# Score units against the last chunk at 448 columns, with the doubled half block squared again by VectorE

## The chip, the cores and the metric

The kernel runs on one core of one Trainium2 chip. The metric is device time in microseconds (us). The kernel before takes 1192.46 us (median of three runs, 1191.73 to 1192.65).

Engines are named as the profile names them: PE is TensorE, DVE is VectorE, ACT is ScalarE, POOL is GpSimd, SP is SyncE (here a DMA queue). PEld is PE's loading of weights, which overlaps its matmuls.

## The reference

```python
# u, v: (8, 3008, 256); z: (8, 3008, 64); w_in: (256, 2048); w_out: (2048, 256)
scores = matmul(z, z.transpose(0, 2, 1)) / S        # S = 3008
attn   = maximum(scores, 0.0) ** 2
x      = (u * matmul(attn, v)).reshape(B * S, D)
h      = x @ w_in
out    = (h / (1 + exp(-1.702 * h))) @ w_out
```

The scores are symmetric, since both factors are z. The kernel uses this: it computes many blocks once, and transposes them ("turns" them) by DMA for use on the other side of the diagonal.

## The kernel before

The 3008 tokens of a batch are cut into six chunks of 512; the last has 448 tokens, and its last block of 128 rows holds the 64 remaining tokens twice. A score unit is two key blocks (2 x 128) against the queries of one chunk. PE computes it in two row tiles of 64 rows that run side by side, ACT applies Relu, and DVE squares. In the code below, `CB` = 4 blocks make a chunk, `NCH` = 6 chunks and `NU` = 12 pairs of key blocks make a batch; `i` is a chunk of queries, `jp` a pair of key blocks. `...` marks lines left out.

```python
LAST = S - (NCH - 1) * CH      # 448
LFULL = LAST - SREM            # 384

def turned(b, i):              # units of chunk i against the last chunk's queries
    return i < NCH - 1 and (b > 0 or i > 3)

def scores(b, group):
    ...
        turn = turned(b, i) and jp >= NU - 2
        kp, qi = (2 * i + jp - (NU - 2), NCH - 1) if turn else (jp, i)
        m = CB // 2 if folded(b, i) and jp == 2 * i + 1 else CB
        for r in range(2):
            h = slice(r * DQK, (r + 1) * DQK)
            pe.matmul(sc[:, r, :m * P], zt[h, 2 * kp + r, :],
                      zt[h, (qi + 1) * CB - m:(qi + 1) * CB, :], start=True, stop=True)

def square(b, i, jp, sc):
    ...
    act.activation(rl, sc, AF.Relu, scale=csc)
    ...
    dve.tensor_tensor(a, rl, rl, ALU.mult)
    if jp // 2 > i and (turned(b, i) or jp < NU - 2):
        if b and i == 0 and LATE:
            late.append(((jp + 2) % NU, lambda: turn_unit(b, i, jp, a)))
        else:
            turn_unit(b, i, jp, a)         # sp.dma_start_transpose into a "tt" tile
```

Of the kernel before, what the change touches and what calls it, by code (L numbers as in the profile page):

```python
# [11 lines left out]
P = 128  # L12
# [3 lines left out]
def kernel(  # L16
# [13 lines left out]
    AF = mybir.ActivationFunctionType  # L30
    ALU = mybir.AluOpType
# [8 lines left out]
    CH = 512  # L40
    NCH = (S + CH - 1) // CH
    CB = CH // P
    NU = NJ // 2
# [6 lines left out]
    LAST = S - (NCH - 1) * CH  # L50
    LFULL = LAST - SREM

    csc = 16.0
    FSC = csc * csc * float(S) * float(S)

    dve, act, pe, sp, pool = nc.vector, nc.scalar, nc.tensor, nc.sync, nc.gpsimd
# [126 lines left out]
    def width(i):  # L183
        return CH if i < NCH - 1 else LAST
# [28 lines left out]
    def folded(b, i):  # L213

        return i < NCH - 1 and b > 0

    def turned(b, i):

        return i < NCH - 1 and (b > 0 or i > 3)

    def scores(b, group):
        scs = []
        zt = ZT[b]
        for i, jp in group:
            sc = ps2.tile([P, 2, CH], F32, name="sc", tag="ps2")
            turn = turned(b, i) and jp >= NU - 2
            kp, qi = (2 * i + jp - (NU - 2), NCH - 1) if turn else (jp, i)
            m = CB // 2 if folded(b, i) and jp == 2 * i + 1 else CB
            for r in range(2):
                h = slice(r * DQK, (r + 1) * DQK)  # L230
                pe.matmul(  # L231
                    sc[:, r, :m * P], zt[h, 2 * kp + r, :], zt[h, (qi + 1) * CB - m:(qi + 1) * CB, :],
                    start=True, stop=True,
                )
            scs.append(sc)
        return [lambda u_=u_, sc=sc: square(b, *u_, sc) for u_, sc in zip(group, scs)]

    def square(b, i, jp, sc):
        rl = pw.tile([P, 2, CH], F16, name="rl", tag="rl", bufs=3)
        if folded(b, i) and jp == 2 * i + 1:  # L240
            rh = rl[:, :, :CH // 2]
            act.activation(rh, sc[:, :, :CH // 2], AF.Relu, scale=csc)
            dve.tensor_tensor(unit[b, i, jp][:, 1], rh, rh, ALU.mult)
            return
        act.activation(rl, sc, AF.Relu, scale=csc)  # L245
        if folded(b, i) and jp == 2 * i:
            a = pa.tile([P, CB, 2, P], F16, name="a", tag="a", bufs=26)
            unit[b, i, jp] = a
            r4 = rl.rearrange("p r (q c) -> p r q c", q=CB)
            dve.tensor_tensor(a.rearrange("p q r c -> p r q c"), r4, r4, ALU.mult)  # L250
            unit[b, i, jp + 1] = pa.tile([P, 2, 2, CH // 2], F16, name="ad", tag="a", bufs=26)
            sp.dma_start_transpose(
                unit[b, i, jp + 1][:, 0].rearrange("p g (r c) -> p (g r) c", c=P),
                a[:, CB // 2:].rearrange("p q r c -> p (q r c)"),
            )
            return
        a = pa.tile([P, 2, CH], F16, name="a", tag="a", bufs=26)
        unit[b, i, jp] = a
        dve.tensor_tensor(a, rl, rl, ALU.mult)  # L259
        if jp // 2 > i and (turned(b, i) or jp < NU - 2):  # L260
            if b and i == 0 and LATE:
                late.append(((jp + 2) % NU, lambda: turn_unit(b, i, jp, a)))
            else:
                turn_unit(b, i, jp, a)

    def turn_unit(b, i, jp, a):
        cj = jp // 2
        if (b, i, cj) not in TT:
            TT[b, i, cj] = pa.tile([P, CB, CB, P], F16, name="tt", tag="tt", bufs=14)
        k0 = 2 * (jp % 2)  # L270
        sp.dma_start_transpose(
            TT[b, i, cj][:, k0:k0 + 2].rearrange("p r g c -> p (r g) c"),
            a.rearrange("p r c -> p (r c)"),
        )
# [309 lines left out]
    def take(b, n):  # L584
        for post_ in scores(b, [queue.pop(0) for _ in range(n)]):
            post_()
# [17 lines left out]
    for copies in [first_zt(g) for g in range(2)]:  # L604
        copies()
    posts = scores(0, [queue.pop(0) for _ in range(2)])
    turns = []
    for g in (2, 3):
# [8 lines left out]
    for b in range(B):  # L617
# [3 lines left out]
        turn, load = (TURN, LOAD) if b else (TURN0, LOAD0)  # L621
# [92 lines left out]
```

## Time and profile before

| | value | where it is read |
|---|---|---|
| time, span | 1192.46 us, 1190.8 us | times, page |
| PE busy | 1183.7 us, 99% | busy table |
| DVE busy, ACT busy | 820.6 us, 830.5 us | busy table |
| score matmuls in the chain that ended last | 6% | chain of waits |
| PE waiting for other engines | 3.3 us, all in the start | list of waits |

The page's busy table gives each engine's busy time, its share of the span and its instructions:

```profile
PE 1183.7 (99%) x11427; PEld 722.6 (61%) x11427; DVE 820.6 (69%) x1315; ACT 830.5 (70%) x987; POOL 231.9 (19%) x325
```

The page's chain that ended last, by engine and by line (L331 output matmuls, L372 and L473 the feed-forward part, L231 scores):

```profile
PE 98%; ACT 0%; DMA 0%; DVE 0%; issue 0%; SPq 0%; ACTq 0%
PE o L331 40%; PE hg L372 27%; PE st L473 23%; PE sc L231 6%; PE yp L529 2%; DMA zf<-in_z_dram 0%; ACT rl L245 0%; DVE zst L126 0%; DVE a L259 0%; ACT ZT L141 0%; ACT zst L124 0%; DVE y L489 0%; SPq L109 0%; PE zp L133 0%; ACTq L245 0%
```

The list of waits of PE (who waited for whom, us in total, times, longest):

```profile
PE w L97 <- DVE nil L75: 1.2, 1, 1.2
PE zp L133 <- DVE zst L126: 1.2, 2, 0.8
PE sc L231 <- ACT ZT L141: 0.9, 3, 0.4
```

PE is busy nearly throughout, waits only at the very start, and is itself nearly the whole chain. So PE's own columns set the time.

The timeline of PE at 238 us (start, us, engine, line, output and inputs, shapes, count) shows what a pair costs. The 18 output matmuls of 64x448 start at 238.19 and the next scores at 239.90, which is 1.71 us for nine pairs, 190 ns a pair. The score pair of 64x512 starts at 237.98 and what follows it at 238.19.

```profile
237.98 0.38 PE L231 MATMUL sc<-ZT 64*128 64x512 f16 x2
238.19 1.86 PE L331 MATMUL o<-a,V 64*128 64x448 f16 x18
239.90 0.59 PE L231 MATMUL sc<-ZT 64*128 64x512 f16 x4
```

The groups of instructions, shapes kept apart (count, busy us, mean ns of one, idle time before them), for Relu (L245, L242) and squares (L259, L243):

```profile
L245 ACT ACTIVATE rl<-sc 128x1024 f16<-128x1024 f32 x309 | 303.5, 1027 | 150.3 <-PE sc L231 147.5 <-DVE a L259 0.8
L259 DVE TENSOR_TENSOR a<-rl 128x1024 f16<-128x1024 f16 x274 | 188.7, 693 | 158.5 <-ACT rl L245 158.1 <-DMA tt<-a 0.4
L242 ACT ACTIVATE rl<-sc 128x512 f16<-128x512 f32 x35 | 21.5, 614 | 7.3 <-PE sc L231 7.3
L243 DVE TENSOR_TENSOR ad<-rl 128x512 f16<-128x512 f16 x35 | 14.7, 420 | 5.9 <-ACT rl L242 5.4
```

### The profile page before, as it was taken

The numbers are of one execution on the slowest core, as the hardware profiler recorded it, in microseconds if no ns is written. First come the engines' busy times: TensorE is split into PE (matmuls) and PEld (weight loads), VectorE is DVE, ScalarE is ACT, GpSimd is POOL, SyncE is SP. The second block draws the span as 40 slices with busy tenths as digits, with TensorE's granted clock in tenths as the row PEclk, the third lists the DMA queues.
The fourth block names the chain that finished last, engine by engine and source line by source line (L and its number), as shares of the span: only waits on it lengthen the run. The fifth ranks groups of instructions, "written<-read, shape, count | busy, mean of one in ns | idle before, by whom it ended". The sixth has DMA issues, their size and how long they took to land.

```text
span 1190.8 us, 27541 instructions
## 1 busy us (share of the span) xinstructions
PE 1183.7 (99%) x11427; PEld 722.6 (61%) x11427; DVE 820.6 (69%) x1315; ACT 830.5 (70%) x987; POOL 231.9 (19%) x325
## 2 busy tenths in 40 slices
PE   8999999999999999999999999999999999999998
PEld 3446765467754676546765478554775547855577
DVE  6788755777757775587765877558776487664776
ACT  7887865688656886478864787657876578672785
POOL 5243100331012320133101331014200142001000
PEclk9999999999999999999999999999999999999999
DMA  9996567666787667856778558886579855695012
GB/s 230 175 137 110 127 138 130 86 112 134 143 132 79 107 141 151 130 68 102 158 140 131 72 95 159 157 112 89 104 128 164 115 88 109 138 165 96 1 37 72
DMA packets 373021, 141.80 MB, mean 119 GB/s; under 512 B 315424, under 2 KB 366368, under 8 KB 372896
## 3 DMA queue, kind: packets, MB, share of 16 engines
q1 hardware_dynamic: 314256, 96.77, 45.1%
q0 software_dynamic: 57280, 42.03, 23.0%
q8 instruction: 89, 1.46, 0.5%
q10 hardware_dynamic: 1360, 1.25, 0.3%
q14 instruction: 36, 0.29, 0.1%
HBM read 60.29 MB, written 24.64 MB: 71 GB/s over the span
## 4 chain that ended last, share of the span: by engine, by line
PE 98%; ACT 0%; DMA 0%; DVE 0%; issue 0%; SPq 0%; ACTq 0%
PE o L331 40%; PE hg L372 27%; PE st L473 23%; PE sc L231 6%; PE yp L529 2%; DMA zf<-in_z_dram 0%; ACT rl L245 0%; DVE zst L126 0%; DVE a L259 0%; ACT ZT L141 0%; ACT zst L124 0%; DVE y L489 0%; SPq L109 0%; PE zp L133 0%; ACTq L245 0%
## 5 line engine op out<-in xcount | busy, mean ns | idle before, releaser
L380 ACT ACTIVATE gf<-hg 128x1024 f32<-128x1024 f32 (+1 forms) x384 | 385.8, 1005 | 138.0 <-PE hg L372 114.7
L245 ACT ACTIVATE rl<-sc 128x1024 f16<-128x1024 f32 x309 | 303.5, 1027 | 150.3 <-PE sc L231 147.5
L331 PEld LDWEIGHTS <-V 64*128 64x128 f16 (+1 forms) x4052 | 239.6, 94 | 235.4 <-issue 13.0
L372 PE MATMUL hg<-xt,W 128*128 128x512 f16 (+1 forms) x1408 | 354.6, 374 | 0.0
L384 DVE TENSOR_SCALAR gt<-gf 128x1024 f16<-128x1024 f32 (+1 forms) x320 | 223.2, 698 | 136.8 <-ACT gf L380 134.1
L331 PE MATMUL o<-a,V 64*128 64x512 f16 (+3 forms) x2286 | 303.8, 369 | 0.0
L259 DVE TENSOR_TENSOR a<-rl 128x1024 f16<-128x1024 f16 x274 | 188.7, 693 | 158.5 <-ACT rl L245 158.1
L193 POOL DMA_DIRECT2D uq<-in_u_dram x188 | 128.5, 691 | 612.2 <-PE sc L231 329.1
L331 PE MATMUL o<-tt,V 64*128 64x512 f16 (+1 forms) x1510 | 234.4, 377 | 0.0
L372 PEld LDWEIGHTS <-W 128*128 128x128 f16 x1536 | 139.3, 98 | 119.3 <-issue 2.6
L473 PEld LDWEIGHTS <-gt 128*128 128x128 f16 x2816 | 169.5, 98 | 31.8
L473 PEld LDWEIGHTS <-s 128*128 128x128 f16 x2112 | 127.8, 98 | 25.3 <-issue 0.3
L231 PE MATMUL sc<-ZT 64*128 64x512 f16 (+1 forms) x688 | 121.6, 367 | 1.2 <-ACT ZT L141 0.9
L473 PE MATMUL st<-WT,gt 128*128 128x128 f16 x1408 | 93.0, 219 | 0.0
L473 PE MATMUL st<-WT,s 128*128 128x128 f16 x1408 | 92.3, 219 | 0.0
L473 PE MATMUL st<-W,gt 128*128 128x128 f16 x1408 | 92.3, 219 | 0.0
L489 DVE SCALAR_TENSOR_TENSOR y<-st,uP 128x256 f32<-128x256 f32 x132 | 55.0, 419 | 21.6 <-PE st L473 10.9
L382 ACT ACTIVATE gt<-gf 128x1024 f16<-128x1024 f32 (+1 forms) x64 | 66.0, 1031 | 2.1
L348 DVE TENSOR_TENSOR xt<-o,ut 128x512 f16<-128x512 f32 x80 | 51.4, 683 | 22.7 <-PE o L331 22.7
L231 PEld LDWEIGHTS <-ZT 64*128 64x128 f16 x688 | 39.0, 94 | 45.0 <-issue 9.1
L483 ACT ACTIVATE uP<-st 128x256 f32<-128x256 f32 x132 | 49.7, 377 | 23.2 <-PE st L473 11.2
L446 DVE TENSOR_TENSOR s<-s,gt 128x1024 f16<-128x1024 f16 x88 | 60.3, 685 | 1.0
(51 smaller groups left out, 618.2 us busy)
## 6 DMA issues: line engine op xcount, KB each, us to landing
out_dram<-y SPq DMA_DIRECT2D x40, 512.0 KB, 3.3
uq<-in_u_dram POOLq DMA_DIRECT2D x156, 128.0 KB, 3.6
V<-in_v_dram POOLq DMA_DIRECT2D x35, 256.0 KB, 6.7
tt<-a SPq DMA_TRANSPOSE x232, 3.8
uq<-in_u_dram POOLq DMA_DIRECT2D x32, 112.0 KB, 5.2
vst<-in_v_dram SPq DMA_DIRECT2D x3, 512.0 KB, 5.8
out_dram<-y POOLq DMA_DIRECT2D x4, 384.0 KB, 3.2
zst<-in_z_dram POOLq DMA_DIRECT2D x7, 192.0 KB, 8.2
```

The source lines that it names most:

```text
L193: eng.dma_start(uq[k * QW:(k + 1) * QW, :n // QW].rearrange("t q c k -> t q (c k)"), src[:, :, cs])
L231: pe.matmul(sc[:, r, :m * P], zt[h, 2 * kp + r, :], zt[h, (qi + 1) * CB - m:(qi + 1) * CB, :], start=True, stop=True,)
L245: act.activation(rl, sc, AF.Relu, scale=csc)
L259: dve.tensor_tensor(a, rl, rl, ALU.mult)
L331: ins = pe.matmul(acc[c][:, :n], V16[b][h, j].rearrange("p (c k) -> p k c", k=NCC)[:, c], weights(b, i, j)[h], start=(k, m) == first[c], s ...
L372: pe.matmul(hg[:, e, :n], W1[:, c, ff * P:(ff + 1) * P], XT[b, i][:, c, :n], start=(c == 0), stop=(c == NCC - 1),)
L380: act.activation(gf[:, :, :n], hg[:, :, :n], AF.Gelu_apprx_sigmoid, scale=1.0 / FSC)
L382: act.activation(g, gf[:, :, :n], AF.Copy, scale=FSC)
L384: dve.tensor_scalar(g, gf[:, :, :n], FSC, None, ALU.mult)
L446: dve.tensor_tensor(s_, ST[b, k, "S1", h], a11, ALU.subtract)
L473: pe.matmul(bank[:, m, :], lhs()[:, f, m, :], right[:, ff, :], start=name in ("P1", "P2", "P5") and m == 0 and ff == 0, stop=ff == NFF // ...
L489: dve.scalar_tensor_tensor(y[:, :, o, c], ST[b, k, "bank" + x], 1.0 / FSC, ST[b, k, "after" + u_], ALU.mult, ALU.add,)
```

## The change

A unit against the last chunk's queries has only 448 different columns; the kernel before computes 512, the last 64 twice. The change computes 448. Where the unit is turned, the doubled half block is still needed by the transpose, and DVE squares it a second time out of the same Relu output.

```diff
-            m = CB // 2 if folded(b, i) and jp == 2 * i + 1 else CB
+            q0, q1 = qi * CH, qi * CH + width(qi)
+            if folded(b, i) and jp == 2 * i + 1:
+                q0 += CH // 2
             for r in range(2):
                 h = slice(r * DQK, (r + 1) * DQK)
                 pe.matmul(
-                    sc[:, r, :m * P], zt[h, 2 * kp + r, :], zt[h, (qi + 1) * CB - m:(qi + 1) * CB, :],
+                    sc[:, r, :q1 - q0], zt[h, 2 * kp + r, :], zt[h].rearrange("d n p -> d (n p)")[:, q0:q1],
                     start=True, stop=True,
                 )
@@
-        act.activation(rl, sc, AF.Relu, scale=csc)
+        turn = turned(b, i) and jp >= NU - 2
+        n = width(NCH - 1 if turn else i)
+        act.activation(rl[:, :, :n], sc[:, :, :n], AF.Relu, scale=csc)
@@
-        dve.tensor_tensor(a, rl, rl, ALU.mult)
+        dve.tensor_tensor(a[:, :, :n], rl[:, :, :n], rl[:, :, :n], ALU.mult)
+        if turn:
+            twice = rl[:, :, LFULL:LAST]
+            dve.tensor_tensor(a[:, :, LAST:], twice, twice, ALU.mult)
```

## The prediction

> **What bounds the kernel.** TensorE, almost everywhere. The page's busy table gives PE 1183.7 us of a span of 1190.8 (99%), DVE 820.6, ACT 830.5. The chain that ended last is 98% PE; score matmuls (line 231) are only 6.2%. In the list of waits PE waits for other engines for 3.3 us in all, every time in the start. The granted clock is 0.999. So PE is paced by its own columns: in the chain, 50 output matmuls of 64x512 (25 pairs; the two row tiles of a pair run side by side) take 5.40 us, 216 ns a pair. In the timeline at 238 us, 9 pairs of 64x448 take 1.71 us, 190 ns a pair. This agrees with the Trainium skill, "TensorE: Matmul & The Clock Gate", section "Wait — 56ns, not 53.3ns?": N / 2.4 GHz + about 2.5 ns between matmuls, here per pair.
>
> **What the change does.** The instruction order shows 96 score units (192 of 688 score matmuls) going from 512 to 448 columns: 72 turned units (10 in each of batches 1 to 7, 2 in batch 0) and 24 units of the last chunk as its own queries. The number of PE instructions does not change.
> - PE: 96 x (216 - 189.5) = 2.5 us less, all on the chain. All 96 stand among row-tiled output pairs, so no mode of the array changes.
> - ACT: Relu over 896 instead of 1024 elements. From 1027 ns for 1024 and 614 for 512 the slope is 0.807 ns: 0.10 us less each, about 10 us of busy time in all. Off the chain.
> - DVE: the square of 1024 takes 693 ns, of 512 takes 420: slope 0.53 ns, fixed part about 147 ns. The 896-wide square should take 625 ns, the added 128-wide one about 215. A turned unit then costs about 840 ns (+147), a last-chunk unit 625 (-68): 72 x 147 - 24 x 68 = +9 us, so DVE goes to about 830 us. Off the chain.
> - DMA transposes of turned units: same number and size, each starting some 0.05 us later. No wait of PE for a transpose is in the list of waits, so this should be hidden.
>
> **On the critical path.** Only the 2.5 us of PE columns (0.2%). The doubled squaring costs nothing unless DVE is late somewhere.
>
> **Predicted time: 1190.0 us**, 8 times in 10 within 1188.9 to 1191.5. Chances: faster by over 2% 0.005, within 2% 0.985, slower by over 2% 0.01. Faster by something: 0.9, since the three runs before spread by only 0.9 us.
>
> **What would show it.** Right: span and PE busy both lower by about 2.5 us; 192 score matmuls of 64x448, start to start 190 ns per pair; PE waits unchanged, none for DVE or a transpose; DVE busy about +9 us with 72 squares near 215 ns; ACT about -10 us. Wrong: PE busy down by 2.5 us but the span less, with PE waiting for DVE squares, transposed tiles or a score bank; or 64x448 score pairs still at 216 ns, because a weight load (94 ns each, two per pair) or the semaphore wait in front of a pair sets the pace.
>
> **What would make it wrong.** A place where the extra DVE instruction (about 0.15 us) holds the three-deep Relu buffer and so ACT, a score bank and PE: today ACT waits for a square only once, 0.8 us. Or the non-contiguous 2x448 operands costing DVE or ACT more than the slope says. Or the time outside the span (1192.46 against 1190.8) moving by as much as the gain.

## More of the kernel before

All transposes go through one queue, SP's, in the order in which `turn_unit` is called. And in chunk 2 of batch 0, PE reads the blocks of its own chunk first, then the turned ones of chunks 0 and 1, then the rest:

```python
def attend(b, i, both=False):
    ...
    if b == 0 and i == 2:
        js = js[own:own + CB] + js[:own] + js[own + CB:]
```

Last, a view that the prediction did not use. It is the view of the tile `tt`, the turned blocks, cut to its transposes (duration of an issue in ns, minimum, median, maximum) and to the time from issue to landing:

```profile
L271 SPq DMA_TRANSPOSE tt<-a x232: 1231/1288/5162, 10.3 to 1087.7; - x116
DMA to landing us min/median/max: 3.1/3.8/10.4
```

An issue usually holds the queue for 1.3 us and lands after 3.8 us, but some hold it for 5 us and land after 10. In the trace, the three slowest landings and the four longest issues are all of transposes issued in the first 56 us. PE did not wait for any of them in this one execution.

## The result, and the profile after

The changed kernel took 1192.36 us (median of six runs, 1189.90 to 1196.78), the kernel before 1192.51 (six runs, 1191.72 to 1192.87). The ratio is 1.0003, with a 95% interval of 0.998 to 1.0027. A ratio here is the mean time of one kernel's fast runs over that of the other's of the same rounds, so it is not quite the ratio of the medians. The median lies outside the predicted range of 1188.9 to 1191.5.

The six runs are not spread around 1192.4, though. Sorted, they are 1189.90, 1190.10, 1190.13, and then 1194.58, 1194.79, 1196.78. Half of them sit where the prediction put them, the other half are 4 to 7 us above, and none is near the median. All six count as fast, since a run is called slow only from 1.5% on. So the ratio averages over two groups, and the first question is what separates them.

The profiled execution was the slowest one. The busy table of the changed kernel (its span is 1195.0 us). PE's 1182.9 us contains matmuls at half clock, of which more below, so it can't be compared with 1183.7 as it stands:

```profile
PE 1182.9 (99%) x11427; PEld 723.2 (61%) x11427; DVE 825.0 (69%) x1387; ACT 821.2 (69%) x987; POOL 231.2 (19%) x325
```

Its list of waits of PE:

```profile
PE o L338 <- DMA tt<-a: 5.4, 1, 5.4
PE w L97 <- DVE nil L75: 1.2, 1, 1.2
PE sc L233 <- ACT ZT L141: 0.7, 2, 0.4
PE zp L133 <- DVE zst L126: 0.6, 1, 0.6
PE st L480 <- ACT uP L490: 0.2, 1, 0.2
```

Two waits are new: 5.4 us for a turned tile, and 0.2 us for ACT, which the timeline puts at 109.8 us. The small one is in eight of the nine traces of the changed kernel and its edited forms (all but the one whose score matmuls are set back to 512 columns) and in no trace of the kernel before without the second squaring. The large one is what matters here. The timeline of PE shows when, first the same place in the kernel before, where the ninth of the 64x512 matmuls on `tt` (the first that needs the turned blocks of chunk 1) starts at 41.81 us without a wait, then the changed kernel:

```profile
40.73 0.81 PE L331 MATMUL o<-tt,V 64*128 64x512 f16 x6
41.59 1.03 PE L331 MATMUL o<-tt,V 64*128 64x512 f16 x8
```

```profile
40.37 0.38 PE L338 MATMUL o<-tt,V 64*128 64x512 f16 x2
46.16 1.46 PE L338 MATMUL o<-tt,V 64*128 64x512 f16 x6 [5.41 <-DMA tt<-a]
47.41 0.63 PE L233 MATMUL sc<-ZT 64*128 64x512 f16 x2
...
58.12 0.37 PE L233 MATMUL sc<-ZT 64*128 64x448 f16 x2
```

The chain that ended last names the transfer, issued at 36.34 us and landed 9.77 us later:

```profile
35.83 0.51 ACT rl L249
36.34 9.77 DMA tt<-a
46.11 0.05 issue
46.16 1.46 PE o L338 x6
```

The Relu in front of the transfer is only what the chain inferred. The block of this transfer had been squared at 27.0 us, and its issue began when the issue before it ended (35.0 + 1.3 us): it stood in the queue.

The view of the tile `tt`, as above:

```profile
L278 SPq DMA_TRANSPOSE tt<-a x232: 1231/1287/6188, 10.5 to 1091.9; - x116
DMA to landing us min/median/max: 3.1/3.6/13.9
```

Three things are to be seen. The wait is at 41 to 46 us, in chunk 2 of batch 0, for the turned blocks of chunk 1. The first matmul that the change touches, the first one of 64x448, starts at 58.12 us, twelve microseconds after the wait has ended. And after the wait the same matmuls take longer: three pairs and a score pair take 1.46 and 0.63 us, from first start to last end, where the timeline of the kernel before has 0.81 and 0.38. The windows view shows why (PE busy first; the granted clock and the DMA share are in front of the last column), first the kernel before, then the changed one:

```profile
44.00:51.00 7.00, 6.96 (x66) 3.42 (x64) 4.45 (x7) 5.05 (x6) 0.99 (x2) 1.00 1.26 173
```

```profile
44.00:51.00 7.00, 4.84 (x24) 1.78 (x26) 0.69 (x1) 1.02 (x1) 0.00 (x0) 0.53 1.19 162
```

The clock was granted at about half in this stretch. The clock's records put it at 0.5 from 44.4 to 51.2 us. The Trainium skill, "TensorE: Matmul & The Clock Gate", section "What's actually happening", says that the array falls back to half its clock after an idle window of about 3.4 us; this trace agrees: PE was idle for 5.4 us, and the clock fell 3.6 us after its last matmul had ended (40.8 us). From 46.2 to 51.2 us the half clock costs about 2.5 us more. An execution of the changed kernel without the wait (the first experiment) has a span of 1186.9, so the slow one is 8.1 us longer, of which 5.4 + 2.5 = 7.9 are now named.

What the change itself does went as predicted, but for the sum of DVE's busy time (below). The groups of the changed kernel:

```profile
L249 ACT ACTIVATE rl<-sc 128x896 f16<-128x896 f32 x96 | 86.1, 916 | 45.1 <-PE sc L233 43.4
L263 DVE TENSOR_TENSOR a<-rl 128x896 f16<-128x896 f16 x96 | 59.8, 624 | 55.9 <-ACT rl L249 55.3
L266 DVE TENSOR_TENSOR a<-rl 128x128 f16<-128x128 f16 x72 | 15.7, 218 | 0.0
L233 PE MATMUL sc<-ZT 64*128 64x448 f16 x192 | 32.4, 349 | 0.0
```

The start-to-start time of a score pair, taken from the trace over all units, has a median of 216 ns at 512 columns (309 units before) and of 189 ns at 448 (96 units after).

### The profile page after: what moved, and what is told of

It is laid out like the page before. It is cut to its first block, busy times and chain, and to the rows that moved or that the text cites. A ratio compares the mean times of both kernels' runs of the same rounds, so it can differ in the third digit from the quotient of the medians.

```text
span 1195.0 us, 27613 instructions
## 1 busy us (share of the span) xinstructions
PE 1182.9 (99%) x11427; PEld 723.2 (61%) x11427; DVE 825.0 (69%) x1387; ACT 821.2 (69%) x987; POOL 231.2 (19%) x325
## 3 DMA queue, kind: packets, MB, share of 16 engines
q8 instruction: 89, 1.46, 0.5%
## 4 chain that ended last, share of the span: by engine, by line
PE 97%; ACT 1%; DMA 1%; DVE 1%; issue 0%; DVEq 0%; ACTq 0%
PE o L338 39%; PE hg L379 27%; PE st L480 23%; PE sc L233 6%; PE yp L536 2%; ACT rl L249 1%; DMA tt<-a 1%; PE w L97 0%; ACT ZT L141 0%; DVE a L263 0%; DVE ut L200 0%; ACT gf L387 0%; ACT zst L124 0%; DVE WT L426 0%; DVE WT L427 0%
## 5 line engine op out<-in xcount | busy, mean ns | idle before, releaser
L249 ACT ACTIVATE rl<-sc 128x1024 f16<-128x1024 f32 (+1 forms) x309 | 294.9, 991 | 163.2 <-PE sc L233 117.9
L263 DVE TENSOR_TENSOR a<-rl 128x1024 f16<-128x1024 f16 (+1 forms) x274 | 183.0, 671 | 158.9 <-ACT rl L249 158.1
L233 PE MATMUL sc<-ZT 64*128 64x512 f16 (+2 forms) x688 | 119.3, 361 | 1.1 <-ACT ZT L141 0.7
```

Source lines behind the costliest of these rows:

```text
L233: pe.matmul(sc[:, r, :q1 - q0], zt[h, 2 * kp + r, :], zt[h].rearrange("d n p -> d (n p)")[:, q0:q1], start=True, stop=True,)
L249: act.activation(rl[:, :, :n], sc[:, :, :n], AF.Relu, scale=csc)
L263: dve.tensor_tensor(a[:, :, :n], rl[:, :, :n], rl[:, :, :n], ALU.mult)
```

## The experiments

The theory (A): the start of batch 0 holds a race that both kernels have. The turned blocks of chunk 1 for chunk 2 come through a queue that runs late in a crowded start, and PE needs them at about 40.5 us. If they are late, the execution is in the slow group. The change has no part in it. The rival (B): the change itself, through its doubled squaring or its narrower instructions, makes executions slow. The instruction order supports A before any run: up to the first unit of 448 columns, all five engines have the same instructions with the same waits in both kernels. It can't say what the placement of a program in memory might do, and so runs are needed.

Fifteen runs were made, in four calls; three of them are of a kernel without an edit. The kernels of one call ran on one chip, beside eleven executions of the kernel before; each call had another chip. All gave correct results.

### The changed kernel again

No edit.

> The changed kernel once more, unedited. Theory A (race in the start): its executions fall into two groups again, fast ones near 1190 us and slow ones of 1193 to 1197 us, and the slow ones lose the time in the first 60 us, in one wait of PE for a transposed tile; the kernel before has such executions too, only more rarely seen. Theory B (the change itself): PE waits appear at changed instructions, that is after 55 us of the span, and never in the kernel before. Theory C (nothing but chance of one chip): all executions near 1190 us now.

Measured: 1188.66, 1188.69, 1190.53, 1194.55, 1195.29 and 1196.37 us. Two groups again, three and three. The kernel before beside it now had slow executions too: 1195.86, 1197.21 and 1198.43 among eleven. Rival B, in which that kernel never has any, falls with this. The profiled execution was a fast one, with a span of 1186.9 us, and PE waited for no turned tile in it:

```profile
PE w L97 <- DVE nil L75: 1.2, 1, 1.2
PE zp L133 <- DVE zst L126: 1.0, 2, 0.6
PE sc L233 <- ACT ZT L141: 0.8, 3, 0.4
PE st L480 <- ACT uP L490: 0.2, 1, 0.2
```

Its busy table, without half clock after the start, has PE at 1179.8 us, where the three traces of the unedited kernel before have 1182.8 to 1183.7:

```profile
PE 1179.8 (99%) x11427; PEld 721.8 (61%) x11427; DVE 823.9 (69%) x1387; ACT 821.2 (69%) x987; POOL 229.9 (19%) x325
```

### The transposes needed first, moved forward in the queue

Two transposes that are needed only for chunk 4 stand in the queue before the two that chunk 2 needs. The edit puts them behind, in the changed kernel and in the kernel before. (In all these edits the list `held` starts empty; that line is left out.)

```diff
+            elif b == 0 and i == 0 and jp >= 8:
+                held.append(lambda: turn_unit(b, i, jp, a))
             else:
                 turn_unit(b, i, jp, a)
+                while (b, i, jp) == (0, 1, 5) and held:
+                    held.pop(0)()
```

> The changed kernel with two transposes of batch 0 (chunk 0 for chunk 4, not needed before about 75 us) moved behind the two of chunk 1 for chunk 2, which then are issued some 6 us earlier (near 27 to 30 us instead of 33 to 38). Theory A: the wait of PE at 41 us goes, all executions lie within 1189.3 to 1191 us, median 1190.0. Theory B: still two groups, as slow executions do not come from there.

> The same two transposes moved in the kernel before. Theory A: no execution slower than 1193 us, median as the kernel before, 1192.3 us (its usual execution has no wait there to lose), and so 2.4 us above the changed kernel with the same edit. Theory B: the same, but the changed kernel with that edit does not get below it in all executions.

Measured: the changed kernel 1188.40 to 1190.28 us, median 1188.87, ratio 0.9963 (0.9943 to 0.9982) against the unedited kernel before. The kernel before with the edit 1191.15 to 1193.66, median 1192.80, ratio 0.999 (0.997 to 1.001). Neither has an execution in the slow group, though 1193.66 is a little above the bound that was set, and four of the changed kernel's six lie below the lower bound of 1189.3. With the race mostly out of both, the change is worth the mean of 1192.47 less that of 1189.18, 3.3 us, from six runs each. That is 0.8 more than predicted. Part of it may be the start: in the two traces, the kernel before has half clock from 8.5 to 11.9 us and the changed one has not.

### The same transposes, moved back

The kernel before, without the change, with its two critical transposes four places later.

```diff
+            elif b == 0 and i == 1 and jp < 6:
+                held.append(lambda: turn_unit(b, i, jp, a))
             else:
                 turn_unit(b, i, jp, a)
+                while (b, i, jp) == (0, 1, 9) and held:
+                    held.pop(0)()
```

> The kernel before, with the two transposes of chunk 1 for chunk 2 moved four places later in the queue (behind chunk 1 for chunk 4). Theory A: they land near 45 to 47 us instead of 35 to 37, PE waits for them 4 to 6 us from 41 us on, and all executions are 4 to 8 us slower, 1196 to 1200 us: the slow group, made on purpose in a kernel without the change. Theory B: no lasting effect, under 2 us.

Measured: 1198.25 to 1203.03 us, ratio 1.0053 (1.0028 to 1.0077). All six are in the slow group, and two of them (1201.38 and 1203.03) above the range that was expected. From the trace, the two landed at 43.9 and 44.8 us. Its list of waits of PE, and the timeline:

```profile
PE o L336 <- DMA tt<-a: 4.1, 1, 4.1
```

```profile
44.87 1.46 PE L336 MATMUL o<-tt,V 64*128 64x512 f16 x6 [4.12 <-DMA tt<-a]
```

So the slow group can be made on purpose, in a kernel that lacks the change, by delaying these two transposes alone. The half clock follows here as well, until 50.7 us. The wait of 4.1 and half of the 5.8 us after it make 7.0 us, and the span of 1196.9 is 7.0 above that of a wait-free execution of the kernel before (1189.9, below).

### The kernel before again, twice

No edit.

> The kernel before, unedited, for its distribution and, with luck, a trace of a slow execution of it. In the runs so far 3 of its 17 executions took 1195.9 to 1198.4 us, the others 1191.4 to 1192.9. Theory A (race in the start): about a fifth to a half of these executions are slow again, and if the traced one is slow, it shows one wait of PE for a transposed tile near 41 us, as the changed kernel's slow trace did. Theory B (the change itself): no slow execution here.

> The kernel before, unedited, one look, for a trace of a slow execution: a third of its executions so far are slow (11 of 34). If this one is: one wait of PE of 4 to 6 us for a transposed tile near 41 us, before any instruction that the change touches. If it is fast, nothing follows.

Measured: the first gave 1191.70, 1192.36, 1195.89, 1196.30, 1198.68 and 1198.90 us, four slow of six; its profiled execution was the fast 1191.70, with a span of 1189.9 us. The second gave one execution, of 1192.69 us, which is not of the slow group; a full-sized slow trace of the kernel before was not caught. But that trace holds a small version of the same wait at the same place (list of waits, then timeline):

```profile
PE o L331 <- DMA tt<-a: 1.1, 1, 1.1
```

```profile
41.80 0.82 PE L331 MATMUL o<-tt,V 64*128 64x512 f16 x6 [1.08 <-DMA tt<-a]
```

The tile landed at 41.8 us. So even within what looked like one tight level of the kernel before, an execution can carry 1.1 us of this wait. Counting all five sets of rounds and these two runs, the unedited kernel before had 16 of 57 executions over 1194 us; the changed one had 6 of 12 over 1194. The first six of the kernel before, those that stood beside the changed kernel in the result, happened to hold none.

### The columns alone, and the doubled squaring alone

Both have the two transposes moved forward. In the first, the changed kernel gets its 512 columns back on PE, while Relu and squares stay narrow. In the second, the kernel before gets the second squaring and nothing else.

```diff
-            q0, q1 = qi * CH, qi * CH + width(qi)
+            q0, q1 = qi * CH, (qi + 1) * CH
```

```diff
         dve.tensor_tensor(a, rl, rl, ALU.mult)
+        if turned(b, i) and jp >= NU - 2:
+            twice = rl[:, :, LFULL:LAST]
+            dve.tensor_tensor(a[:, :, LAST:], twice, twice, ALU.mult)
```

> The changed kernel with the two transposes moved, and its score matmuls back at 512 columns; Relu and squares stay narrow, the doubled squaring stays. If PE columns are the whole gain: back at the level of the kernel before with the same move, 1191.2 to 1193 us, 2.5 us above the narrow one (1188.4 to 1190.3). If narrower Relu or squares are worth something: between the two.

> The kernel before with the two transposes moved and the second squaring of the doubled half block added, everything else at full width: 72 more instructions on VectorE, about 15.5 us of its busy time. If the second squaring costs nothing, as predicted: 1191.2 to 1193.7 us, as without it. If it holds up PE through the Relu buffer or the transposes: 1 us or more above that, with PE waits after 55 us.

Measured, columns restored: 1191.12 to 1192.77 us, mean 1191.64. The same kernel at 448 columns has a mean of 1189.18, so the columns are worth 2.5 us, as predicted. It was run on another chip. The spans of the two profiled executions, neither with a wait for a turned tile, say the same: 1189.3 against 1186.8. The narrower Relu and squares by themselves gave nothing that is clear of the spreads: the wide kernel's mean is 0.8 us below that of the kernel before with the same move (1192.47), and its traced span of 1189.3 is near the 1189.9 of a wait-free trace of the kernel before.

Measured, doubled squaring alone: 1191.82 to 1194.58 us, mean 1192.84, against 1192.47 for the kernel before with the same move of transposes. One of six is above the expected 1193.7. A cost of 0.4 us is not clear of these spreads. DVE's busy time is 838.7 us: here the second square starts 34 ns after the end of the first, which writes the same columns, and the two take 951 ns, against 760 in the changed kernel. So this run asks more of DVE than the change does. In the list of waits PE has two small new ones: the 0.2 us for ACT that the changed kernel has too, and 0.3 us, which the timeline puts at 1092 us, in the last batch:

```profile
1092.40 0.82 PE L339 MATMUL o<-tt,V 64*128 64x512 f16 x6 [0.30 <-DMA tt<-a]
```

So the squaring is hidden but for these two places. The second, where a turned tile is needed just as it lands, shows in no trace of the changed kernel.

### Filler matmuls in the start

Among the fast executions there are two levels about 1.2 us apart (1188.6 and 1190.1 for the changed kernel). Some traces have the granted clock at half from about 8 to 11 us, as that of the kernel before has (7.9 to 11.3), and others not. The edit puts three matmuls of zeros into the gaps ahead of that (cut: the lines that keep the tile `warm` of the first warm-up matmuls).

```diff
     for g in (2, 3):
         first_cast(g)
+        for _ in range(g - 1):
+            pe.matmul(warm, nil[:, :P], nil, start=True, stop=True)
         turns.append(first_zt(g))
```

> The changed kernel with the two transposes moved and three filler matmuls in the idle gaps of PE at 6 to 8 us. In traces, the granted clock falls to half from 8 to 11 us in the executions of the upper of two levels (1.2 us apart: 1188.6 and 1190.1 here) and not in those of the lower. If those gaps make the clock fall: all executions at the lower level, 1188.2 to 1189.2 us. If not: two levels as before.

Measured: 1188.23, 1188.57, 1188.62, 1189.51, 1190.72 and 1193.43 us. The expectation failed: there is no single level, and one execution is 5 us above it. The traced execution had no half clock, but so have most without the edit. Whether the fillers help is open; they were dropped. The second trace of the kernel before, above, shows that the small wait for a turned tile can make a difference of this size too, and not only the clock.

### The transposes in the order in which they are needed

Four transposes for chunk 4 stand behind those for chunks 2 and 3, in both kernels.

```diff
+            elif b == 0 and i < 2 and jp >= 8:
+                held.append(lambda: turn_unit(b, i, jp, a))
             else:
                 turn_unit(b, i, jp, a)
+                while b == 0 and (i, jp) in ((1, 7), (2, 7)) and held:
+                    held.pop(0)()
```

> The changed kernel with batch 0's transposes in the order in which they are needed: those for chunk 4 (four of them) behind those for chunks 2 and 3. With the two of the first edit moved, 2 of 30 executions (4 kernels with it, 24 timed, and the traces) were still 3 to 5 us over their kernel's low level. If a late tile for chunk 2 or 3 is all that the slow group is: every execution within 1188.2 to 1190.5 us.

> The kernel before with the same order of transposes: every execution within 1190.9 to 1193.3 us. The changed kernel with this order is then 2.5 us below it (ratio 0.9979), as the prediction had it for the change, now with the race taken out of both.

Measured: the changed kernel 1188.26, 1188.61, 1188.63, 1188.66, 1190.89 and 1191.44 us, so two of six miss the bound of 1190.5. The kernel before 1191.14 to 1192.86, within its bounds. The medians are 1188.65 and 1191.42 us, the means 1189.41 and 1191.63: the change gains 2.8 us by the one and 2.2 by the other. The trace of the kernel before is instructive: its queue ran as late as in the slow trace of the changed kernel, and the tenth transpose landed at 45.8 us, against 46.1 there. In the old order the tenth is the one that chunk 2 waits for. In the new order that one is the eighth and landed at 37.0, and PE did not wait.

### The last batch's scores taken earlier

The doubled squaring had met one just-in-time tile in the last batch. The edit takes the last four score units earlier, on top of the order above.

```diff
-    SCHED_LAST = SCHED | {3: {n: 1 for n in (14, 34)} | {NJ: 2}, 4: {NJ: 2}, 5: {}}
+    SCHED_LAST = SCHED | {3: {n: 1 for n in (6, 14, 22, 28)}, 4: {NJ: 2}, 5: {}}
```

> The changed kernel with that order of transposes, and in the last batch the last four score units before chunk 4 taken at steps 6, 14, 22 and 28 of chunk 3 instead of 14, 24, 24 and 34, so that the last turned tile lands 1.3 us earlier (in the traces it lands within 0.1 us of PE's need at 1086 to 1094 us, and 0.3 us late with the doubled squaring alone). If that place costs time: 0.1 to 0.3 us below the kernel without this edit; if not: the same.

Measured: 1188.91 to 1190.49 us, median 1189.59, no better than without (1188.65). Its lowest execution is 0.65 us above the lowest without the edit. The trace again has a wait in the start, with the tile landing at 41.1 us (list of waits):

```profile
PE o L343 <- DMA tt<-a: 0.9, 1, 0.9
```

The edit was dropped.

### More time on the reader's side

PE reads the turned blocks of chunk 1 eight steps, 1.7 us, later, with and without the new order of transposes.

```diff
-            js = js[own:own + CB] + js[:own] + js[own + CB:]
+            js = js[own:own + 2 * CB] + js[:CB] + js[own + 2 * CB:-CB + 1] + js[CB:own] + js[-CB + 1:]
```

> The changed kernel with the transposes of batch 0 in the order needed, and PE reading the tiles of chunk 1 for chunk 2 eight steps (1.7 us) later. In the last call a trace with the first edit alone still had a wait of 0.9 us there, and 2 of 6 executions of it were 2.3 and 2.8 us over its low level. If the rest comes from the same place: none over 1190.2 us (low level 1188.3 to 1188.7 plus 1.2 us for a half-clock window at the start), and no wait of PE for a transposed tile between 35 and 60 us in the trace. If it comes from elsewhere: one to three of six at 1190.8 to 1192 again.

> The same two edits in the kernel before: none over 1193 us, low level 1191.2 us; the changed kernel with both edits 2.5 to 2.8 us below it, ratio 0.9977 to 0.9979 with a narrow interval.

> The changed kernel with PE's later reading alone, the transposes in their old order. In the slow trace the tile landed 5.4 us late, in another of the kernel before 1.1 us late. If lateness is all there is to the slow group: small stalls (up to 1.7 us) vanish and large ones shrink by 1.7 us: slow executions at 1191.5 to 1194 us instead of 1194.5 to 1196.8, the rest at 1188.3 to 1190 us.

Measured, both edits on the changed kernel: 1188.21 to 1189.95 us, mean 1189.03, as expected, and no wait for a turned tile in the trace. Both edits on the kernel before: 1191.41 to 1193.12 us but for one of 1197.14, so its expectation failed. The medians of the two, 1188.79 and 1192.12 us, differ by 3.3 us where 2.5 to 2.8 was expected. Reading later alone, on the changed kernel: 1188.81, 1188.94, 1190.75, 1191.57, 1191.76 and 1201.07 us. The last one, which was profiled, is the slowest of all of the changed kernel's, and not one of the shrunken slow ones that were expected. The two traces, from the list of waits, the kernel before with both edits first:

```profile
PE o L336 <- DMA tt<-a: 1.6, 1, 1.6
```

```profile
PE o L338 <- DMA tt<-a: 9.2, 1, 9.2
```

The tiles landed at 44.2 and at 53.1 us. The lateness of this queue has a long tail, and the remedies take most executions out of it, not all. Counted as more than 3 us above the lowest execution of the same kernel, 22 of 69 executions of the two unedited kernels are slow, and 3 of 60 of the ten kernels with transposes moved forward.

Over all seventeen traces, the landing of the last tile of chunk 1 for chunk 2 and PE's wait go together. In eight, all with transposes moved forward, it landed from 32.9 to 37.0 us and PE did not wait. The other nine (landings from the trace, waits from the list of waits, all us):

| kernel in the trace | landed | PE waited | span |
|---|---|---|---|
| changed, again | 35.0 | 0 | 1186.9 |
| before, of the prediction | 37.2 | 0 | 1190.8 |
| before, again (first) | 40.7 | 0.2, from the timeline | 1189.9 |
| changed, last batch's scores earlier | 41.1 | 0.9 | 1188.1 |
| before, again (second) | 41.8 | 1.1 | 1190.9 |
| before, both edits | 44.2 | 1.6 | 1191.3 |
| before, transposes moved back | 44.8 | 4.1 | 1196.9 |
| changed, with the result | 46.1 | 5.4 | 1195.0 |
| changed, reading later | 53.1 | 9.2 | 1199.3 |

The kernels with later reading need the tile about 1.7 us later than the others, so their waits are shorter for the same landing. The trace of the kernel before on which the prediction rests was lucky in this respect and unlucky in another: half clock from 7.9 to 11.3 us.

## Why the prediction was right or wrong

**What bounds the kernel: right.** PE's columns. Restoring the 64 columns gives the time back, 2.46 us by the means and 2.5 by the spans; nothing else that the change does can be told from zero.

**The size of the gain: right.** Predicted 96 x 26.5 ns = 2.5 us on PE. Measured 27 ns per pair (216 to 189), 96 of them, 2.6 us. The fast executions of the changed kernel in the result, 1189.90 to 1190.13, are the predicted 1190.0. That they agree to 0.2 us is partly luck: the record gives these three a granted clock of 0.999, as it does the profiled execution of the kernel before, while the two best of the changed kernel's later runs have 1.000 and took 1188.7. Group against group, the executions of the two unedited kernels under 1194 us have means of 1189.7 (6) and 1192.1 (41), 2.4 us apart, and medians 1.7 apart.

**ACT: right.** Predicted about 10 us less, measured 830.5 to 821.2. No effect on the time.

**DVE: right in each instruction, off in the sum.** Predicted 625 and 215 ns, measured 624 and 218. But the second squaring starts 83 ns before the first one's end, in all 72 cases, so a turned unit costs 66 ns more and not 147. The prediction added two durations that overlap. By 66 ns the sum is 72 x 66 - 24 x 69 = +3.1 us, not +9; measured, the engine's busy time rose by 4.4 us between these two traces, where traces of the unedited kernel before differ among themselves by 2.6 (820.1 to 822.7). On the changed kernel's PE it costs at most the 0.2 us at 109.8 us; the 0.3 us in the last batch were seen only with the squaring added to the full-width kernel.

**The transposes: this step failed, though not as an effect of the change.** The prediction says "No wait of PE for a transpose is in the list of waits, so this should be hidden", and it built its narrow range on "the three runs before spread by only 0.9 us". Both readings are of few executions: one trace and three times. In the trace, the critical tile landed 4.6 us before PE needed it (37.2 against 41.8 us), and a list of waits does not show a margin. In another execution of the very same kernel it landed 1.1 us late, and 16 of 57 took over 1194 us, against a median of 1192.6; that the wait is in those too is inferred from their times and from the runs that moved it. So the start holds a race that was already there. The three changed runs that hit it moved the median by 2.3 us (the three fast ones have 1190.10), about as much as the change gains, and the six runs of the kernel before that stood beside it happened to miss it. The wait ended 12 us before the first changed instruction, the same slow group was made in the unchanged kernel by delaying two transposes, and moving them forward took it out of nearly all executions of both kernels: the cause is shown. That the change makes the race no likelier (6 of 12 against 16 of 57) follows from the identical instructions up to that point, but the counts are too few to show it by themselves.

**What would make it wrong.** The list looked for a place where the change makes DVE late. PE waiting for turned tiles was named among the signs, but as an effect of the change; a wait that belongs to the old kernel was not thought of.

**What stays open.** What makes the queue late in one execution and not in another. In the slow trace single issues held it for up to 6.2 us; the blocks had long been squared (at 27.0 us for the one that was issued at 36.3 and landed at 46.1). The DMA share of all ten-microsecond windows from 10 to 50 us is above 1.1 in both kernels' traces, with the loads of v and u in flight. The Trainium skill, "DMA: Bandwidth & Descriptors", section "Issuing engines are not separate DMA queues", says that transfers started by any engine run on the same 16 DMA engines and interleave. That fits, but no run here took the loads away, so the contention is argued and not shown.

**The version to keep.** The changed kernel with batch 0's transposes moved forward beats both: means of 1189.0 to 1189.4 us in three forms (two transposes moved; all in the order of need; the same and read later), ratios of 0.9963 to 0.9965 against the kernel before of the same rounds, each with an interval that ends below 1. These ratios hold both the change (about 2.5 us) and the rarer race.

## What to carry to other kernels

A profile shows waits, not margins: before an effect of a few microseconds is predicted, look also at how long before its use each DMA lands, above all in the start, where all loads crowd together. When the runs of one kernel fall into two groups, compare group with group and find what separates them, before a mean or a median is read; and count enough executions of the old kernel to know whether it has the groups too. In a queue that works in order, the order of issue should be the order of need.

## What the Trainium skill lacked or had wrong

- "DMA: Bandwidth & Descriptors", section "Latency and other measured facts", gives no spread for a DMA transpose beside other traffic. Here the same 256 KB transpose (128x1024 of 2 bytes) landed after 3.1 us at the least, 3.6 in the median and 13.9 at the most within one execution, and its issue held the queue for 1.2 to 6.2 us.
- "Perfetto Trace Analysis", section "Optimization Strategy", says to find the gaps on the busiest engine and what they wait for. The gap was absent from the trace of the kernel before and 1.1 us long in another trace of the same kernel; the page does not say to look at margins, or at more than one execution.
- "TensorE: Matmul & The Clock Gate", section "What's actually happening", was borne out for a long wait: half clock for 6.8 us around one of 5.4 us. No figure of the page says how much of a window must be idle for the clock to fall. In three traces here it fell at 7.9 to 8.5 us after a stretch of 3.4 us at full clock in which PE had been idle for only 1.4 to 1.6 us (before; before with two transposes moved forward; changed, reading later); in a fourth (before, in the order of need) 1.4 us of 3.4 left it full.
